# Scores of six half-sequences as 64-row matmuls in both row halves of TensorE, in three units of four PSUM banks

## The chip, the cores and the metric

One core of one Trainium2 chip runs the whole kernel. The metric is the device time of one execution in microseconds, median of several runs. The engines are named as in the profile: PE (TensorE matmuls), PEld (its weight loads), DVE (VectorE), ACT (ScalarE), POOL (GpSimd) and SP (SyncE, which here only issues DMAs).

## What is computed

Attention with a window of 96 keys and 8 global keys, with a linear bias per head, and behind it a gated feed-forward network (FFN) on the heads put side by side.

```python
batch, n_heads, seq, head_dim = (4, 8, 768, 64)
n_global, n_local = (8, 96)
...
scores = q @ k.T / sqrt(64) - slope[h] * dist
keep = (key < 8) | ((0 <= query - key) & (query - key < 96))
a = softmax(where(keep, scores, -1e9))
x = (a @ v), heads side by side            # 3072 x 512
out = (relu(x @ w_gate) * (x @ w_val)) @ w_out    # 512 -> 1536 -> 512
```

## The kernel before

**Tiling.** The 3072 queries are eight halves `s` of 384 (four sequences, two halves each); `s % 2` tells an even half from an odd one, and the halves three to eight of the title are `s` = 2 to 7. The keys lie in tiles of 120 with the 8 global keys ahead of them. Queries are taken in three interleaved sets (NN = 3), so a key tile that serves w positions makes 3w score columns per head. `banks_of_half` puts the key tiles that a half needs into three groups `g`, each a PSUM bank of scores for two heads: in an even half 432, 432 and 288 + 48 columns, in an odd one 144 + 336, 384 + 96 and 432 columns. The eight heads are four pairs `p`; a pair's q and k lie in 128 partitions, head `e` = 0 in the lower 64 and `e` = 1 in the upper 64.

**Scores before.** One matmul computes both heads of a pair: the weights are `kT` of the pair (128 rows), and the moving operand is a padded q (`qTb`) in which each head's columns have zeros in the other head's 64 rows. `piece_qk` (L396) does it for one group in one bank of `qk_psum`, puts the exponential on ACT (L413) and leaves the multiplication by the mask (`piece_mask`, L428, DVE) to be issued later.

**AV, normalization.** `piece_av` (L444) multiplies one head's exponentials by `vbuf`, which also holds ones, so the row sums come out beside the values; ACT takes their logarithm (L453) and, for both heads of a pair, the inverse as exp(-ln) (L458); `piece_norm` (L464, DVE) multiplies it into `xT`, the FFN's input. A head's exponentials of all its key tiles have to be there.

**Order of the work.** From half three on, the attention of half `c + 1` is woven by hand into the FFN of half `c`. `weave` (L769) walks through FFN items of equal weight (24 gate and value products, then the output products) and issues each attention item when its place has come; `spread` gives the places evenly. `attention_pieces` (L509) is the list: three banks of scores for pair 0, three for pair 1, the two AV of pair 0, and so on, 26 items. A stage has 35 FFN items, 31 where `c` = 6. Each engine then works strictly in the order of issue.

**PSUM.** Eight banks: three in `qk_psum`, two in `av_psum`, three in `ff_psum` (gate, value and output products). A gate's bank comes free with ACT's relu (L709), a value's bank with DVE's product (L716).

**Input of the halves four to eight.** `early_pieces` (L389) for half `c + 2`: POOL casts k into `kc` (L366) and q, with zeros between, into `qz` (L374); SP transposes them by DMA into `kNb` (L377) and `qTb` (L381); POOL orders the keys into `kT`. Half three is cast on POOL and transposed on PE in the setup weave (`T2_piece`, L942).

The heart of the scores before:

```python
ps = qk_psum.tile([128, 512], FP32, name="qk_ps")
...
nc.tensor.matmul(ps[:, c : c + n_], lhsT=kt[:, j, :],
                 rhs=qd[:, :, :, a : a + w], start=True, stop=True)
```

Of the kernel before, what the change touches and what calls it, by code (L numbers as in the profile page):

```python
# [8 lines left out]
FP32 = mybir.dt.float32  # L9
BF16 = mybir.dt.bfloat16  # L10
# [6 lines left out]
def kernel(  # L17
# [23 lines left out]
    NN = 3  # L41
# [24 lines left out]
    const = ctx.enter_context(tc.tile_pool(name="const", bufs=1))  # L66
    setupp = ctx.enter_context(tc.tile_pool(name="setupp", bufs=1))
    stage = ctx.enter_context(tc.tile_pool(name="stage", bufs=1))
    es_pool = ctx.enter_context(tc.tile_pool(name="es", bufs=3))
    rc_pool = ctx.enter_context(tc.tile_pool(name="rc", bufs=2))  # L70
    xt_pool = ctx.enter_context(tc.tile_pool(name="xt", bufs=3))
    ht_pool = ctx.enter_context(tc.tile_pool(name="ht", bufs=2))
# [14 lines left out]
    kT = [[const.tile([128, NT, 128], BF16, name=f"kT{i}_{p}") for p in range(HP)] for i in range(2)]  # L87
    qTb = [const.tile([128, HP, 2, QH], BF16, name=f"qT{i}") for i in range(2)]
    kNb = [const.tile([128, HP, QH], BF16, name=f"kN{i}") for i in range(2)]
    qz = [const.tile([128, NN, HP, 2, 128], BF16, name=f"qz{i}") for i in range(2)]  # L90
    kc = [const.tile([128, NN, DM], BF16, name=f"kc{i}") for i in range(2)]

    obuf = const.tile([128, 2, 5, DM // 2], FP32)
# [149 lines left out]
    def warm_up(n):  # L243
        wps = ff_psum.tile([128, 512], FP32, name="ff_ps")
        for _ in range(n):
            nc.tensor.matmul(wps, lhsT=warm, rhs=warm.unsqueeze(1).to_broadcast([128, 4, 128]), start=True, stop=True)

    xT_of = {}
    es_of = {}
    es01_of = {}  # L250
    av_of = {}

    cast_of = {}
# [91 lines left out]
    def piece_exp(s, p, g):  # L345
        if p == HP - 1:

            es = kNb[s].rearrange("d p t -> d (p t)")[:, 480 * g : 480 * (g + 1)]
        else:
            if g == 0:  # L350
                es01_of[s, p] = es_pool.tile([128, 2, 480], BF16, name="es01")
            es = es01_of[s, p][:, g] if g < 2 else es_pool.tile([128, 480], BF16, name="es2")
# [9 lines left out]
        for g in range(3):  # L362
            piece_exp(s, p, g)

    def piece_cast_k(s, p):
        nc.gpsimd.tensor_copy(  # L366
            kc[s % 2].rearrange("t n (h d) -> t h n d", d=D)[:, 2 * p : 2 * p + 2],
            ks_of[s][:, 2 * p : 2 * p + 2, :].rearrange("t e (n d) -> t e n d", n=NN))
# [7 lines left out]
    def piece_xk(s, n):  # L376
        nc.sync.dma_start_transpose(  # L377
            out=kNb[s % 2][:, :, n * 128 : (n + 1) * 128], in_=kc[s % 2][:, n])

    def piece_xq(s, n):  # L380
        nc.sync.dma_start_transpose(  # L381
            out=qTb[s % 2].rearrange("d p e t -> d (p e) t")[:, :, n * 128 : (n + 1) * 128],
            in_=qz[s % 2][:, n].rearrange("t p e z -> t (p e z)"))

    def piece_order(s, p):
        b, half = divmod(s, 2)
        put_keys(nc.gpsimd.tensor_copy, nc.gpsimd.tensor_copy, kT[b % 2][p], kNb[s % 2][:, p], half)

    def early_pieces(s):  # L389
        out = [(0.0, lambda p=p: piece_cast_k(s, p)) for p in range(HP)]  # L390
        out += [(0.0, lambda n=n: piece_xk(s, n)) for n in range(NN)]
        out += [(0.0, lambda p=p: piece_cast_q(s, p)) for p in range(HP)]
        out += [(0.0, lambda n=n: piece_xq(s, n)) for n in range(NN)]
        out += [(0.0, lambda p=p: piece_order(s, p)) for p in range(HP)]
        return out

    def piece_qk(s, p, g, later=None):
        b, half = divmod(s, 2)
        kt = kT[b % 2][p]
        qd = qTb[s % 2][:, p].rearrange("d e (n p) -> d e n p", n=NN)  # L400
        bank = banks_of_half[half][g]
        cols = sum(2 * NN * w for _, _, w, _ in bank)
        ps = qk_psum.tile([128, 512], FP32, name="qk_ps")
        if g == 0:
            es01_of[s, p] = es_pool.tile([128, 2, 480], BF16, name="es01")
        es = es01_of[s, p][:, g] if g < 2 else es_pool.tile([128, 480], BF16, name="es2")
        c = 0
        for j, a, w, m in bank:
            n_ = 2 * NN * w
            nc.tensor.matmul(ps[:, c : c + n_], lhsT=kt[:, j, :],  # L410
                             rhs=qd[:, :, :, a : a + w], start=True, stop=True)
            c += n_
        nc.scalar.activation(es[:, 0:cols], ps[:, 0:cols], AF.Exp, bias=0.0, scale=scale)  # L413
# [90 lines left out]
    def piece_mul_wide(s, p):  # L504
        if s not in xT_of:
            xT_of[s] = xt_pool.tile([128, N_DC, QH], BF16, name="xT")
        nc.vector.tensor_tensor(xT_of[s][:, p, :], av_of[s, p][1][:, 0:QH], av_of[s, p, "r"], op=ALU.mult)

    def attention_pieces(s):  # L509
        masks = []  # L510

        def qk(p, g):
            ready = masks[:]
            masks.clear()
            piece_qk(s, p, g, masks)
            for f in ready:
                f()

        def flush():
            for f in masks:  # L520
                f()
            masks.clear()

        QK = lambda p: [(0.18, lambda g=g: qk(p, g)) for g in range(3)]
        AV = lambda p: [(0.29, lambda e=e: (flush(), piece_av(s, p, e))) for e in range(2)]
        N = lambda p: [(0.0, lambda: piece_norm(s, p, 1))]
        g = QK(3)
        a = AV(2)
# [161 lines left out]
    def ffn_pieces(c):  # L690
# [63 lines left out]
        if c == NHALF - 2:  # L754
            return f1, pair.items({"1": late[0:2], "2": late[2:4]})

        space = qz[0].rearrange("t n p e z -> t (n p e z)").bitcast(FP16)
# [35 lines left out]

    for h in range(H):
        setup_sid(h)
    QKB, FFB, AVB = (qk_psum, "qk_ps"), (ff_psum, "ff_ps"), (av_psum, "av_ps")

    def AV(s, p, *pools):
        piece_av_wide(s, p, *pools)
        piece_norm_wide(s, p)  # L800
# [202 lines left out]
```

The softmax here doesn't subtract the row's maximum and nothing guards it: scores larger than these inputs give would overflow.

## Time and profile before

| | us |
|---|---|
| median of 7 runs | 242.06 (241.84 to 243.29) |
| the profiled execution | 242.33 |
| its span | 240.2 |
| granted TensorE clock, share of full | 1.0 in all slices |
| DMA | 32.37 MB, mean 135 GB/s |

The stages, by the start of each half's first gate product in the timeline of PE:

| stage | start | length | attention in it |
|---|---|---|---|
| FFN of half 3 (`c` = 2) | 77.46 | 26.68 | half 4 (odd) |
| `c` = 3 | 104.14 | 27.01 | half 5 (even) |
| `c` = 4 | 131.15 | 27.78 | half 6 (odd) |
| `c` = 5 | 158.93 | 27.00 | half 7 (even) |
| `c` = 6 | 185.93 | 25.09 | half 8 (odd) |
| `c` = 7 | 211.02 | to the end | none |

The attention of half 3 lies in the weave before 77 us, beside the last FFN items of the first two halves. In a row of the groups, the columns are the line, the engine, the operation, output and inputs with their shapes, the count; then the busy time, the mean duration of one, and the idle time of the engine just before them with what ended it. Durations of matmuls overlap: a matmul lasts until its last result is written, and the next one starts earlier.

### The profile page before, as it was taken

Reading aid. Unit: us, or ns where it says so; the run is one execution under the profiler, and the core shown is the slowest. Engines: PE = TensorE matmul, PEld = TensorE weight load, DVE = VectorE, ACT = ScalarE, POOL = GpSimd, SP = SyncE. Lnnn points to the kernel's source line nnn. Section 1 sums busy time; section 2 is a strip of 40 time slices with the busy share of each in tenths; the row PEclk is TensorE's granted clock in tenths of the full one; section 3 lists DMA queues with packets and bytes.
Section 4 is the critical chain, followed back from the end, with each engine's and each line's share of the span. In section 5 each row is a group of like instructions: output and inputs, shape, how many; then the busy total and the mean of one; then the engine's idle time right before and its main releaser. Section 6 shows DMA issues by size and latency. Waiting matters only on the chain.

```text
span 240.2 us, 5192 instructions
## 1 busy us (share of the span) xinstructions
PE 232.5 (97%) x1859; PEld 156.2 (65%) x1859; DVE 175.4 (73%) x443; ACT 154.5 (64%) x328; POOL 95.3 (40%) x213
## 2 busy tenths in 40 slices
PE   7889999999999999999999999999999999999993
PEld 4675765666558666776658666676658666766682
DVE  6877676767877769485895779675985867964783
ACT  7999855878662787538854787547764888433300
POOL 8998934924591068103484056502560000000000
PEclk9999999999999999999999999999999999999999
DMA  6999999997979956928659755929451200020004
GB/s 167 206 172 185 206 287 255 151 106 256 133 172 153 290 134 134 93 91 261 91 111 128 217 165 131 114 78 297 70 131 45 90 0 3 0 87 3 0 25 151
DMA packets 78329, 32.37 MB, mean 135 GB/s; under 512 B 55424, under 2 KB 76928, under 8 KB 78304
## 3 DMA queue, kind: packets, MB, share of 16 engines
q0 software_dynamic: 34896, 10.27, 38.1%
q1 hardware_dynamic: 43408, 21.78, 34.0%
q8 instruction: 14, 0.23, 0.4%
q14 instruction: 11, 0.09, 0.1%
HBM read 28.38 MB, written 6.29 MB: 144 GB/s over the span
## 4 chain that ended last, share of the span: by engine, by line
PE 81%; DMA 9%; POOL 6%; issue 2%; DVE 0%; POOLq 0%; DVEq 0%
PE ff_ps L700 46%; PE ff_ps L590 15%; PE ff_ps L733 9%; DMA ks<-in_k_dram 6%; PE av_ps L444 6%; PE qk_ps L410 6%; DMA vbuf<-in_v_dram 3%; POOL vbuf L151 1%; POOL kc L128 1%; POOL wg L168 1%; POOL qT L192 1%; PE qk_ps L296 1%; DVE obuf L601 0%; POOL obuf L260 0%; POOL wv L168 0%
## 5 line engine op out<-in xcount | busy, mean ns | idle before, releaser
L700 PE MATMUL ff_ps<-xT,wv 128*128 128x384 bf16 x384 | 77.7, 326 | 0.1
L700 PE MATMUL ff_ps<-xT,wg 128*128 128x384 bf16 x384 | 77.7, 326 | 0.0
L709 ACT ACTIVATE grelu<-ff_ps 128x384 bf16<-128x384 f32 x96 | 46.7, 490 | 45.5 <-PE ff_ps L700 32.9
L716 DVE TENSOR_TENSOR ht<-ff_ps,grelu 128x384 f16<-128x384 f32 x96 | 53.1, 554 | 24.5 <-PE ff_ps L700 12.4
L700 PEld LDWEIGHTS <-wv 128*128 128x128 bf16 x384 | 36.2, 97 | 22.4 <-DMA wv<-in_moe_w_val_dram 0.5
L700 PEld LDWEIGHTS <-wg 128*128 128x128 bf16 x384 | 36.0, 97 | 20.8 <-issue 0.5
L464 DVE TENSOR_TENSOR xT<-av_ps,rcp 64x384 bf16<-64x384 f32 x48 | 26.6, 555 | 24.8 <-ACT rcp L458 24.0
L413 ACT ACTIVATE es<-qk_ps 128x432 bf16<-128x432 f32 (+2 forms) x78 | 40.8, 532 | 5.7 <-PE qk_ps L410 3.7
L428 DVE TENSOR_TENSOR es<-es,m_all 128x432 bf16<-128x432 bf16 (+5 forms) x118 | 33.6, 329 | 0.2
L366 POOL CAST kc<-ks 128x384 bf16<-128x384 f32 x20 | 9.6, 525 | 57.6 <-DMA ks<-in_k_dram 57.6
L453 ACT ACTIVATE lnd<-av_ps 64x384 f32<-64x384 f32 x48 | 23.3, 485 | 9.0 <-PE av_ps L444 8.5
L410 PE MATMUL qk_ps<-qT,kT 128*128 128x432 bf16 (+5 forms) x118 | 26.6, 286 | 0.1
L151 POOL DMA_DIRECT2D vbuf<-in_v_dram x29 | 24.7, 861 | 0.1
L601 DVE TENSOR_TENSOR obuf<-ff_ps,obuf 128x512 f32<-128x512 f32 (+1 forms) x35 | 20.5, 592 | 4.4 <-PE ff_ps L590 2.1
L733 PE MATMUL ff_ps<-wo_sb,ht 128*128 128x512 f16 x96 | 22.8, 378 | 0.0
L444 PEld LDWEIGHTS <-vbuf 128*128 128x128 bf16 x216 | 18.3, 98 | 6.8
L444 PE MATMUL av_ps<-es,vbuf 128*128 128x216 bf16 (+4 forms) x216 | 21.4, 226 | 0.0
L590 PEld LDWEIGHTS <-hsum 128*128 128x128 f16 x168 | 16.4, 98 | 2.0
L410 PEld LDWEIGHTS <-kT 128*128 128x128 bf16 x118 | 11.4, 98 | 7.7
L590 PE MATMUL ff_ps<-wo_sum,hsum 128*128 128x256 f16 x126 | 14.9, 273 | 0.0
L590 PEld LDWEIGHTS <-ht 128*128 128x128 f16 x144 | 13.7, 97 | 1.8
L733 PEld LDWEIGHTS <-ht 128*128 128x128 f16 x96 | 8.7, 97 | 8.7
(125 smaller groups left out, 246.1 us busy)
## 6 DMA issues: line engine op xcount, KB each, us to landing
out_dram<-obuf SPq DMA_DIRECT2D x22, 256.0 KB
ks<-in_k_dram SPq DMA_DIRECT2D x5, 768.0 KB
qs<-in_q_dram SPq DMA_DIRECT2D x5, 768.0 KB
vbuf<-in_v_dram POOLq DMA_DIRECT2D x23, 120.0 KB, 4.6
wv<-in_moe_w_val_dram POOLq DMA_DIRECT2D x3, 512.0 KB, 9.8
wo_sb<-in_moe_w_out_dram POOLq DMA_DIRECT2D x1, 1536.0 KB, 21.8
wg<-in_moe_w_gate_dram POOLq DMA_DIRECT2D x2, 512.0 KB, 9.7
ks<-in_k_dram SPq DMA_DIRECT2D x4, 192.0 KB
```

Source lines behind the costliest of these rows:

```text
L151: nc.gpsimd.dma_start(out=v_dst(b, NG + r0, NG + r0 + n, j), in_=v[b, :, KT * j + r0 : KT * j + r0 + n, :].rearrange("h p d -> p h d"))
L410: nc.tensor.matmul(ps[:, c : c + n_], lhsT=kt[:, j, :], rhs=qd[:, :, :, a : a + w], start=True, stop=True)
L413: nc.scalar.activation(es[:, 0:cols], ps[:, 0:cols], AF.Exp, bias=0.0, scale=scale)
L428: nc.vector.tensor_mul(e4, e4, mk)
L444: nc.tensor.matmul(av3[:, :, a : a + w], lhsT=vb[:, j, z0 : z0 + 128], rhs=es[:, c : c + NN * w].rearrange("k (n p) -> k n p", n=NN), star ...
L453: nc.scalar.activation(ln[o0 : o0 + 64], av[d0 : d0 + 64, 0:QH], AF.Ln, bias=0.0, scale=1.0)
L464: nc.vector.tensor_tensor(xT_of[s][r, p, :], av_of[s, p, e][r, 0:QH], av_of[s, p, "r"][r], op=ALU.mult)
L590: nc.tensor.matmul(ps[:, c0 : c0 + DH], lhsT=lhs(i), rhs=rhs(i), start=(i == 0), stop=(i == NP - 1), skip_group_check=True)
L700: nc.tensor.matmul(st[key][:, 0:QH], lhsT=w_of(w, dc, fc), rhs=xT_of[c][:, dc, :], start=(dc == 0), stop=(dc == N_DC - 1))
L709: nc.scalar.activation(gr, psg[:, 0:QH], AF.Relu, bias=0.0, scale=1.0)
L716: nc.vector.tensor_tensor(ht[:, fc, :], psv[:, 0:QH], st["r", fc], op=ALU.mult)
L733: nc.tensor.matmul(ps2, lhsT=ht[:, fc, n * 128 : (n + 1) * 128], rhs=wo_sb[:, fc, :], start=(fc == 0), stop=(fc == N_FC - 1))
```

## The change

- The scores of the halves three to eight (`s` = 2 to 7) no longer use padded q. `score_unit` issues, for each key tile and pair, two matmuls of 64 rows: head `e` takes `kT` and q from the partitions 64e to 64e + 63, and so the rows 64e on of TensorE, and writes to a bank of its own. A bank now holds one head of each of two neighbouring pairs, with the same columns as before.
- Scores are issued in three units of four banks (two groups for both `e`), each one of `av_psum` and three of `qk_psum`. Unit 1 makes groups 0 and 1 of pairs 0 and 1; unit 2 their group 2 and group 0 of pairs 2 and 3; unit 3 the other two groups of pairs 2 and 3.
- `unit_exp` takes the exponential of one bank and leaves its mask to the next step; the list of `attention_pieces` puts the exponentials between the AV of pairs 0 and 1. It has 29 items, four of them empty ("wait").
- q is cast and transposed like k (`piece_cast2`, `piece_x`), without zeros; `qz` and its two memsets go, `qc` comes. The two transposed q buffers `qT2` lie in the one tile `qTb[1]`.
- Half three's q is copied for both heads in one ACT copy.
- `es_pool` has 12 buffers of one bank in place of 3 of two and 3 of one.
- The last attention is spread to 0.88 of its stage, as the others, in place of 0.8. The scratch space of the last output products lies in `qTb[0]`.

```diff
-    es_pool = ctx.enter_context(tc.tile_pool(name="es", bufs=3))
+    es_pool = ctx.enter_context(tc.tile_pool(name="es", bufs=12))
...
-    qz = [const.tile([128, NN, HP, 2, 128], BF16, name=f"qz{i}") for i in range(2)]
+    qT2 = [qTb[1].rearrange("d p e t -> d (p e t)")[:, i * HP * QH : (i + 1) * HP * QH].rearrange(
+        "d (p t) -> d p t", p=HP) for i in range(2)]
+    qc = [const.tile([128, NN, DM], BF16, name=f"qc{i}") for i in range(2)]
...
-    def piece_cast_q(s, p):
-        qsrc = qs_of[s][:, 2 * p : 2 * p + 2, :].rearrange("t e (n d) -> t e n d", n=NN)
-        for e in range(2):
-            nc.gpsimd.tensor_copy(qz[s % 2][:, :, p, e, 64 * e : 64 * e + 64], qsrc[:, e])
+    def piece_cast2(s, p, dst, src):
+        nc.gpsimd.tensor_copy(
+            dst[s % 2].rearrange("t n (h d) -> t h n d", d=D)[:, 2 * p : 2 * p + 2],
+            src[s][:, 2 * p : 2 * p + 2, :].rearrange("t e (n d) -> t e n d", n=NN))
+
+    def piece_x(dst, src, n):
+        nc.sync.dma_start_transpose(out=dst[:, :, n * 128 : (n + 1) * 128], in_=src[:, n])
...
+    def score_unit(s, groups, pools):
+        b, half = divmod(s, 2)
+        out = []
+        for pp, g in groups:
+            banks = []
+            for e in range(2):
+                pool, name = pools.pop(0)
+                banks.append(pool.tile([128, 512], FP32, name=name))
+                out.append((pp, g, e, banks[e]))
+            c = 0
+            for j, a, w, m in banks_of_half[half][g]:
+                for p in (2 * pp, 2 * pp + 1):
+                    for e in range(2):
+                        r = slice(64 * e, 64 * e + 64)
+                        q3 = qT2[s % 2][r, p].rearrange("d (n p) -> d n p", n=NN)
+                        nc.tensor.matmul(banks[e][:, c : c + NN * w], lhsT=kT[b % 2][p][r, j, :],
+                                         rhs=q3[:, :, a : a + w], start=True, stop=True)
+                    c += NN * w
+        return out
+
+    def unit_exp(s, pp, g, e, ps):
+        bank = banks_of_half[s % 2][g]
+        cols = sum(2 * NN * w for _, _, w, _ in bank)
+        es = es_pool.tile([128, 480], BF16, name="es")
+        nc.scalar.activation(es[:, 0:cols], ps[:, 0:cols], AF.Exp, bias=0.0, scale=scale)
+
+        def mask():
...
+                h0 = 4 * pp + e
+                mk = m_all[:, h0 : h0 + 3 : 2, 0 if j == 0 else 1, :, m : m + w]
...
+                nc.vector.tensor_mul(e4, e4, mk)
...
+        return mask
+
     def attention_pieces(s):
...
-        return (QK(0) + QK(1) + AV(0) + N(0) + QK(2) + AV(1) + N(1) + g[0:1] + a[0:1] + g[1:3] + a[1:2]
-                + N(2) + [(0.0, lambda: None)] * 2 + AV(3) + N(3))
+        def x(scored=None):
+            ready = masks[:]
+            masks.clear()
+            if scored:
+                scores(*scored)
+            masks.append(unit_exp(s, *units.pop(0)))
+            for f in ready:
+                f()
+
+        U = [([(0, 0), (0, 1)], (AVB, QKB, QKB, QKB)),
+             ([(0, 2), (1, 0)], (AVB, QKB, QKB, QKB)),
+             ([(1, 1), (1, 2)], (AVB, QKB, QKB, QKB))]
...
+        return (X(U[0]) + X() + X() + X() + wait + X(U[1]) + X() + a0[0:1] + X() + a0[1:2] + N(0) + X() + wait
+                + X(U[2]) + a1[0:1] + X() + a1[1:2] + N(1) + X() + X() + wait + AV(2) + N(2) + wait * 2 + AV(3) + N(3))
...
-    for i in range(2):
-        nc.gpsimd.memset(qz[i].rearrange("t n p e z -> t (n p e z)").bitcast(mybir.dt.uint32), 0)
...
-        piece_copy_q(2, p, nc.scalar.copy)
+        nc.scalar.copy(qT2[0][:, p], tp_of[2, p, 0])
...
-            placed.append(spread(attention_pieces(c + 1), 0.0, 0.88 if c + 2 < NHALF else 0.8))
+            placed.append(spread(attention_pieces(c + 1), 0.0, 0.88))
```

More of the change, by code (lines that the diff above doesn't have):

```diff
@@ L246, in warm_up @@
             nc.tensor.matmul(wps, lhsT=warm, rhs=warm.unsqueeze(1).to_broadcast([128, 4, 128]), start=True, stop=True)
+    QKB, FFB, AVB = (qk_psum, "qk_ps"), (ff_psum, "ff_ps"), (av_psum, "av_ps")
     xT_of = {}
     es_of = {}
-    es01_of = {}
     av_of = {}
@@ L349, in piece_exp @@
         else:
-            if g == 0:
-                es01_of[s, p] = es_pool.tile([128, 2, 480], BF16, name="es01")
-            es = es01_of[s, p][:, g] if g < 2 else es_pool.tile([128, 480], BF16, name="es2")
+            es = es_pool.tile([128, 480], BF16, name="es")
         c = 0
@@ L363, in piece_biased @@
             piece_exp(s, p, g)
-    def piece_cast_k(s, p):
+    def piece_cast2(s, p, dst, src):
         nc.gpsimd.tensor_copy(
-            kc[s % 2].rearrange("t n (h d) -> t h n d", d=D)[:, 2 * p : 2 * p + 2],
-            ks_of[s][:, 2 * p : 2 * p + 2, :].rearrange("t e (n d) -> t e n d", n=NN))
-    def piece_cast_q(s, p):
-        qsrc = qs_of[s][:, 2 * p : 2 * p + 2, :].rearrange("t e (n d) -> t e n d", n=NN)
-        for e in range(2):
-            nc.gpsimd.tensor_copy(qz[s % 2][:, :, p, e, 64 * e : 64 * e + 64], qsrc[:, e])
[L376 to L383, printed above, removed]
+            dst[s % 2].rearrange("t n (h d) -> t h n d", d=D)[:, 2 * p : 2 * p + 2],
+            src[s][:, 2 * p : 2 * p + 2, :].rearrange("t e (n d) -> t e n d", n=NN))
+    def piece_x(dst, src, n):
+        nc.sync.dma_start_transpose(out=dst[:, :, n * 128 : (n + 1) * 128], in_=src[:, n])
     def piece_order(s, p):
@@ L389, in early_pieces @@
     def early_pieces(s):
[L390 to L393, printed above, removed]
+        out = [(0.0, lambda p=p: piece_cast2(s, p, kc, ks_of)) for p in range(HP)]
+        out += [(0.0, lambda n=n: piece_x(kNb[s % 2], kc[s % 2], n)) for n in range(NN)]
+        out += [(0.0, lambda p=p: piece_cast2(s, p, qc, qs_of)) for p in range(HP)]
+        out += [(0.0, lambda n=n: piece_x(qT2[s % 2], qc[s % 2], n)) for n in range(NN)]
         out += [(0.0, lambda p=p: piece_order(s, p)) for p in range(HP)]
@@ L403, in piece_qk @@
         ps = qk_psum.tile([128, 512], FP32, name="qk_ps")
-        if g == 0:
-            es01_of[s, p] = es_pool.tile([128, 2, 480], BF16, name="es01")
-        es = es01_of[s, p][:, g] if g < 2 else es_pool.tile([128, 480], BF16, name="es2")
+        es = es_pool.tile([128, 480], BF16, name="es")
         c = 0
@@ L507, in piece_mul_wide @@
         nc.vector.tensor_tensor(xT_of[s][:, p, :], av_of[s, p][1][:, 0:QH], av_of[s, p, "r"], op=ALU.mult)
-    def attention_pieces(s):
[L510 to L517, printed above, removed]
+    def score_unit(s, groups, pools):
[20 more added lines that the diff above has]
+        cols = sum(2 * NN * w for _, _, w, _ in bank)
+        es = es_pool.tile([128, 480], BF16, name="es")
+        nc.scalar.activation(es[:, 0:cols], ps[:, 0:cols], AF.Exp, bias=0.0, scale=scale)
+        def mask():
+            c = 0
+            for j, a, w, m in bank:
+                n_ = 2 * NN * w
+                e4 = es[:, c : c + n_].rearrange("k (i n p) -> k i n p", i=2, n=NN)
+                h0 = 4 * pp + e
+                mk = m_all[:, h0 : h0 + 3 : 2, 0 if j == 0 else 1, :, m : m + w]
+                if w == WQ:
+                    e4 = e4.rearrange("k i n p -> k i (n p)")
+                    mk = mk.rearrange("k i n p -> k i (n p)")
+                nc.vector.tensor_mul(e4, e4, mk)
+                for i in range(2):
+                    es_of[s, 2 * pp + i, j, e] = (es, c + i * NN * w)
+                c += n_
+        return mask
+    def attention_pieces(s):
+        masks, units = [], []
         def flush():
@@ L522, in flush, with scores @@
             masks.clear()
-        QK = lambda p: [(0.18, lambda g=g: qk(p, g)) for g in range(3)]
-        AV = lambda p: [(0.29, lambda e=e: (flush(), piece_av(s, p, e))) for e in range(2)]
+        def scores(groups, pools):
+            units.extend(score_unit(s, groups, list(pools)))
+        def x(scored=None):
[9 more added lines that the diff above has]
+             ([(1, 1), (1, 2)], (AVB, QKB, QKB, QKB))]
+        X = lambda u=None: [(0.0, lambda: x(u))]
+        AV = lambda p: [(0.0, lambda e=e: (flush(), piece_av(s, p, e))) for e in range(2)]
         N = lambda p: [(0.0, lambda: piece_norm(s, p, 1))]
-        g = QK(3)
-        a = AV(2)
-        return (QK(0) + QK(1) + AV(0) + N(0) + QK(2) + AV(1) + N(1) + g[0:1] + a[0:1] + g[1:3] + a[1:2]
-                + N(2) + [(0.0, lambda: None)] * 2 + AV(3) + N(3))
+        wait = [(0.0, lambda: None)]
+        a0, a1 = AV(0), AV(1)
+        return (X(U[0]) + X() + X() + X() + wait + X(U[1]) + X() + a0[0:1] + X() + a0[1:2] + N(0) + X() + wait
+                + X(U[2]) + a1[0:1] + X() + a1[1:2] + N(1) + X() + X() + wait + AV(2) + N(2) + wait * 2 + AV(3) + N(3))
     out_v = out.rearrange("(s p n) d -> s n p d", p=128, n=NN)
@@ L755, in ffn_pieces @@
             return f1, pair.items({"1": late[0:2], "2": late[2:4]})
-        space = qz[0].rearrange("t n p e z -> t (n p e z)").bitcast(FP16)
+        space = qTb[0].rearrange("d p e t -> d (p e t)").bitcast(FP16)
         across = Pair((c - 1, 2), (c, 2), space.rearrange("t (s c z) -> t s c z", s=4, c=NP))
@@ L795 @@
         setup_sid(h)
-    QKB, FFB, AVB = (qk_psum, "qk_ps"), (ff_psum, "ff_ps"), (av_psum, "av_ps")
     def AV(s, p, *pools):
```

## The prediction

> **What bounds the kernel now.** I read the page first: how busy each engine is, the chain that ended last, the groups of the lines that the change touches.
>
> ```profile
> PE 232.5 (97%) x1859; PEld 156.2 (65%) x1859; DVE 175.4 (73%) x443; ACT 154.5 (64%) x328; POOL 95.3 (40%) x213
> ...
> PE 81%; DMA 9%; POOL 6%; issue 2%; DVE 0%; POOLq 0%; DVEq 0%
> ...
> L413 ACT ACTIVATE es<-qk_ps 128x432 bf16<-128x432 f32 (+2 forms) x78 | 40.8, 532 | 5.7 <-PE qk_ps L410 3.7
> ...
> L410 PE MATMUL qk_ps<-qT,kT 128*128 128x432 bf16 (+5 forms) x118 | 26.6, 286 | 0.1
> ```
>
> TensorE (PE) is busy 97% and makes 81% of the chain; what isn't PE in it lies in the first 40 us, where nothing is changed. Asked from 47 us on, the list of waits holds no wait of PE at all. So from there to the end a microsecond of PE time is a microsecond of the kernel, as long as no new wait arises. A busy sum can't price a matmul, because consecutive matmuls overlap (432 columns last 0.35 us but the next starts 0.18 us later); I price by the distance from one start to the next, in PE's timeline:
>
> ```profile
> 133.70 0.35 PE L410 MATMUL qk_ps<-qT,kT 128*128 128x432 bf16 x1
> 133.88 0.81 PE L700 MATMUL ff_ps<-xT,wv 128*128 128x384 bf16 x4
> 134.53 0.81 PE L700 MATMUL ff_ps<-xT,wg 128*128 128x384 bf16 x4
> 135.18 0.37 PE L410 MATMUL qk_ps<-qT,kT 128*128 128x144 bf16 x2
> 135.39 0.33 PE L700 MATMUL ff_ps<-xT,wv 128*128 128x384 bf16 x1
> ```
>
> Four FFN products of 384 columns take 0.65 us, so 162.5 ns each, which is 2.5 ns and 1 ns per 2.4 columns. By that 432 columns take 182.5 ns (the rows: 0.18) and the bank of 144 and 336 takes 205 (the rows: 0.21).
>
> **What the scores cost now.** Per pair of heads an even half has 432, 432, 288 and 48 columns: 182.5 + 182.5 + 122.5 + 28 (the 48 columns by the start of the next product, 109.69 to 109.72 us) = 515 ns. An odd half has 144, 336, 384, 96 and 432: 62.5 + 142.5 + 162.5 + 42.5 + 182.5 = 592. Four pairs, three halves of each sort: 12 x 0.515 + 12 x 0.592 = 13.3 us.
>
> **What they cost in row halves.** No 64-row product stands in this trace. The nearest row is L479, the AV of the first two halves, which puts two heads side by side in *column* halves:
>
> ```profile
> 25.73 0.48 PE L479 MATMUL qk_ps<-es,ones 128*64 128x72 bf16 x10
> 26.04 0.48 PE L479 MATMUL qk_ps<-es,vbuf 128*64 128x72 bf16 x10
> 26.45 1.47 PE L700 MATMUL ff_ps<-xT,wv 128*128 128x384 bf16 x8
> 27.76 0.81 PE L700 MATMUL ff_ps<-xT,wg 128*128 128x384 bf16 x4
> 28.50 0.50 PE L479 MATMUL av_ps<-es,ones 128*64 128x72 bf16 x10
> 28.84 0.48 PE L479 MATMUL av_ps<-es,vbuf 128*64 128x72 bf16 x10
> ```
>
> Ten matmuls, five pairs of 72, 168, 192, 48 and 216 columns, take 0.31 us (25.73 to 26.04). One after the other they would take 0.58 us for the columns alone. So both matmuls of a pair run at once, at the price of one. The columns per head in an odd half are just these five: 0.308 us for two heads. In an even half (216, 216, 144, 24) it is 92.5 + 92.5 + 62.5 + 28 = 276 ns. Over all: 12 x 0.308 + 12 x 0.276 = 7.0 us, **6.3 us less**.
>
> **What going in and out of the halves costs.** The same rows show it. The ten matmuls from 26.04 should be followed at 26.35; L700 comes at 26.45, and its eight products then take 1.31 instead of 1.30: 0.11 us to leave the mode. On the way in, the four products from 27.76 stream until 28.41, L479 starts at 28.50, and its first ten take 0.34 instead of 0.31: 0.12 us. The other entry, at 25.08, gives 0.12 as well. In the kernel before the halves from three on never change mode. The change has three units in each of six halves, all between 128-row products: 18 entries and 18 exits, 18 x 0.12 + 18 x 0.11 = **4.1 us more**. Two thirds of the gain go here. I take the same price for row halves; the bounds are nothing (switching rows costs no gap) and twice that.
>
> **The weights.** There are twice as many loads, 64 rows by 128 columns. In L479 a pair's two loads of 64 columns fit between pairs 25 ns apart; a 128x128 load fits into the 28 ns of a 24-column product. So 128 columns for both row halves fit in 28 ns if they load together (cost nothing: every pair is at least that long), and in 56 ns if one after the other. Then only the pairs of 24, 48 and 72 columns grow, by 28, 28 and 24 ns: 12 x 28 + 12 x 52 = 1.0 us. I take 0, the L479 row, and keep 1.0. A page of the Trainium skill speaks against the 6.3 us ("TensorE: Matmul & The Clock Gate", Part 3, Measured speedup): four row tiles gave 3.07 times, not four. By that the 7.0 us would be 7.0 / 0.77 = 9.1, the gain 4.2, and switching would eat all of it; the rows above show pairs at full rate, and I go by them.
>
> **New waits.** PE works in order, so a unit that waits for one of its four banks holds up the FFN behind it. An attention item comes after about 1.06 FFN products of 0.65 us (29 items on 0.88 x 35; before, 26). I walked an even half from its start at 0, with relu 0.49, exponential 0.53 to 0.58, mult 0.55 and Ln 0.49 us as in ACT's and DVE's rows, and 0.2 us from a product's last start of a bank to its reader.
> - Unit 1 at 0.65 needs three qk banks and an AV bank, all long free. Its four exponentials share ACT with three relus and end at 4.35.
> - Unit 2 (after the sixth product, 4.45) needs the qk banks of the second to fourth exponential; the last is wanted by its second group alone, at 4.75. Slack 0.35 us.
> - AV of pair 0 (6.3) needs the mask after unit 2's first exponential, done at about 6.1 on DVE. Slack 0.2; before, it needed masks from two banks earlier. This is the tightest place.
> - Unit 3 (11.4) needs an AV bank whose normalization ends near 10.8, and an exponential that ends near 11.4, again for its second group alone. Slack 0.3. AV of pair 1 needs nothing of unit 3.
> - The exponentials now take the AV banks too, but in the walk each is read 0.6 us or more before it is asked for again.
>
> ACT could turn these slacks into stalls, since everything above hangs on it. Its share in the first 24 products of each stage (columns: PE, weight loads, DVE, ACT):
>
> ```profile
> 104.14:123.43 19.29, 19.29 (x138) 12.27 (x136) 15.07 (x37) 14.52 (x31) 6.82 (x19) 1.00 0.69 172
> 131.15:151.14 19.99, 19.96 (x148) 12.80 (x146) 16.18 (x41) 15.16 (x31) 8.33 (x24) 1.00 0.68 171
> ...
> 186.05:206.59 20.54, 20.54 (x159) 13.45 (x157) 16.16 (x44) 16.65 (x34) 0.00 (x0) 1.00 0.08 27
> ```
>
> 75 to 81%. Exponentials and masks keep their number and sizes, so the same work goes into some 0.35 us less: 77 to 83%. No lasting backlog; I put 0.4 us in all for the tight places (bounds 0 and 2.4, the latter 0.4 us in each half). Below nothing this can't go, as PE waits for nothing now.
>
> **Edits at nothing.** The padded q casts (8 of 0.38 us per half on POOL) become 4 of 0.53, the size of the kc rows: POOL works 0.9 us less in each half at 40% load, and nothing but the transposes waits for it. The q transposes stay three DMAs on SP's queue (4.26 us, as for the k ones of half the width), behind the k ones and ahead of only the result stores; in the stage from 104 us they end at 122.3 and their reader starts at 131. Both q buffers now lie in one tile; were it tracked whole, a transpose would wait for unit 3, which is a quarter of a stage earlier. The two memsets (2.7 us) go from in front of POOL's 5.6 us wait for ks and only lengthen that wait. Half three's q copies are four on ACT, not eight (0.47 each), while PE waited there for a cast. Twelve es buffers only remove waits. Spreading the last attention to 0.88 puts its last AV five products ahead of the FFN that needs it, as in the other stages, where the norm ends at 130.27 and the product starts at 131.15: 0.9 us of cover, and what exceeds it would be paid once.
>
> **The sum.** -6.3 + 4.1 + 0 + 0.4 = -1.8 us. The profiled execution has a span of 240.2 and a time of 242.33, 2.1 outside the span, which nothing here touches: 238.4 and 240.5. The median is 242.06, 0.3 below that execution; on it, **240.3 us**. A change can be told from none beyond 0.3%, 0.73 us: 241.33 and 242.79 are the bounds.
>
> **Rivals.**
> 1. *Nothing lost at the switches* (6%). The drain seen is that of column halves; with row halves at no gap the sum is -6.3 + 0.4: 236.2. Against it: PE's outgoing weights must be replaced in all rows either way.
> 2. *The waits take it back* (20%). ACT runs late at unit 2, at AV of pair 0 and unit 3. For it: DVE and ACT already wait on one another (24.0 us of norms on rcp, 6.7 of mults on exponentials), and slack is 0.2 to 0.35 us. At its bound of 2.4 us the sum is +0.2: 242.3. It decides from 0.37 us per half. From that price to half as much again (3.3 us), 241.5 to 243.2.
> 3. *The row halves don't run side by side* (12%). Two matmuls with separate inputs write all 128 partitions of two banks at once, which no row here does; L479 writes 64 each. If they take turns, the columns are as many as before, 13.3 us, and 108 more starts at 2.5 ns add 0.3: the switches come on top, 4.1 + 0.3 + 0.4 = +4.8, **246.9, slower**. It decides from 2.2 us over 108 pairs, 20 ns a pair: at 20 ns above L479's distance the gain is gone. Slower weight loads are the same mechanism, smaller.
>
> **How the numbers follow.** The forecast has 62%: with the loads at 1.0, and waits from 0 to 0.8, it spans 239.9 to 241.7; with switches a fifth cheaper, 239.1. Of its 62, 57 are faster and 5 the same. Rival 1 gives 6 faster; rival 2 gives 2 faster, 11 the same, 7 slower; rival 3, which can be partial, 1 the same and 11 slower. In all 65 faster, 17 the same, 18 slower. The range of 8 in 10 leaves out rival 1 and the full rival 3: 238.8 to 243.2.
>
> **What would show it.** In PE's timeline, score matmuls of 64 rows in pairs 3 ns apart and 92 ns to the next for 216 columns (right) or about 185 (rival 3); some 0.1 us of gap at each edge of a unit (none: rival 1); new waits of PE on es, xT or exponentials from 47 us on, over 2 us in sum (rival 2). The stage from 104.14 to 131.15, 27.0 us, should become 26.7. A forecast of faster is wrong if the pairs are 20 ns late or the waits pass 0.37 us in a half.

## The result, and the profile after

| | before | after |
|---|---|---|
| median, us | 242.16 (31 runs) | 244.21 (243.62 to 245.47, 12 runs) |
| ratio | | 1.0089, 95% interval 1.0075 to 1.0104 |
| span of the profiled execution, us | 240.2 | 241.9 |

The changed kernel is 0.9% slower; 240.3 had been forecast, 0.7% faster. The page of the changed kernel, engines, chain and the groups that answer to those shown of before (scores are L513 and L522 now, AV is L431):

```profile
PE 232.8 (96%) x1967; PEld 152.9 (63%) x1967; DVE 175.4 (73%) x443; ACT 149.2 (62%) x324; POOL 88.2 (36%) x191
...
PE 78%; DVE 9%; ACT 8%; issue 2%; DMA 1%; SPq 0%; DVEq 0%; ACTq 0%
...
L431 PE MATMUL av_ps<-es,vbuf 128*128 128x216 bf16 (+4 forms) x216 | 23.8, 226 | 1.3 <-DVE es L534 1.0
```

The busy sums hardly move, and PE's would tell nothing anyway, since its durations overlap. The chain tells more, though not by these shares alone: DVE and ACT held 0% of it and now hold 17%, 40 us, but 17 of the 40 lie ahead of 47 us, in the setup, where the chain of before ran over DMA and POOL. From 47 to 232 us the chain before was PE alone; now DVE holds 15.7 us of that stretch and ACT 4.5. And AV now waits for `es`; before, it waited for nothing:

```profile
L444 PE MATMUL av_ps<-es,vbuf 128*128 128x216 bf16 (+4 forms) x216 | 21.4, 226 | 0.0
```

The list of waits from 47 us to the end, PE and its weight loads, which was empty but for 0.7 us, is now (columns: who waited for whom, us in all, times, longest):

```profile
PE av_ps L431 <- DVE es L534: 1.0, 4, 0.3
```

```profile
PEld L513 <- issue: 4.1, 13, 0.3
PEld L741 <- issue: 4.1, 22, 0.3
PEld L431 <- issue: 1.8, 6, 0.4
PEld L513 <- DVE ht L757: 1.6, 5, 0.3
```

These lists count only idle time that a record shows whole, and "issue" hides who was late. I therefore added up the distances between matmul starts, beyond what the columns take (1 ns per 2.4 columns and 2.5 ns), from 47 us on. That gives the sum by its terms:

| term, us over six halves | forecast | in the trace after |
|---|---|---|
| scores (13.3 before) | 7.0, so -6.3 | 7.17 in 18 units, so -6.1 |
| gaps into and out of the units | +4.1 | 1.72 + 1.63, and 0.2 at the product behind: +3.5 |
| waits of PE | +0.4 | AV 3.6, gate and value products 1.2, output products 0.25, less 0.4 that stood there before: +4.6 |
| sum | -1.8 | +2.0 |

The span grew by 1.7 rather than 2.0: half three's k landed 0.9 us earlier in this execution (its first cast on POOL starts at 37.04 instead of 37.94), and a PE wait of 0.5 us at 40.47 is gone. The starts bear the sum out: the last gate product ahead of the first unit starts 0.64 us earlier than before (46.26), PE's last product of all 1.49 us later, 2.1 us in between.

**The score unit** works as forecast. PE in the stage of half 5, from 104.16 us:

```profile
104.16 0.81 PE L741 MATMUL ff_ps<-xT,wg 128*128 128x384 bf16 x4
104.90 0.26 PE L513 MATMUL av_ps<-qT,kT 64*128 64x216 bf16 x1
104.91 0.26 PE L513 MATMUL qk_ps<-qT,kT 64*128 64x216 bf16 x1
105.01 0.25 PE L513 MATMUL av_ps<-qT,kT 64*128 64x216 bf16 x1
105.01 0.44 PE L513 MATMUL qk_ps<-qT,kT 64*128 64x216 bf16 x5
105.38 0.82 PE L741 MATMUL ff_ps<-xT,wv 128*128 128x384 bf16 x4
```

Two products of 64 rows start together, into banks of their own, and the next two 0.1 us later. The products from 104.16 stream until 104.81, and the unit starts at 104.90: the gap of 0.1 us in; the gap out is alike.

**Where it is lost** is 17 us further on, at the AV of pair 2. PE, ACT and DVE (POOL and the weight loads are left out):

```profile
120.08 1.13 DVE L451 TENSOR_TENSOR xT<-av_ps,rcp 64x384 bf16<-64x384 f32 x2
...
120.90 0.49 ACT L750 ACTIVATE grelu<-ff_ps 128x384 bf16<-128x384 f32 x1 [0.18 <-PE ff_ps L741]
...
121.25 0.56 DVE L757 TENSOR_TENSOR ht<-ff_ps,grelu 128x384 f16<-128x384 f32 x1
121.29 0.44 ACT L522 ACTIVATE es<-qk_ps 128x336 bf16<-128x336 f32 x1
121.44 0.81 PE L741 MATMUL ff_ps<-xT,wg 128*128 128x384 bf16 x4
...
121.72 0.51 DVE L626 TENSOR_TENSOR hsum<-ht 128x512 f16<-128x512 f16 x1
...
122.09 0.35 PE L431 MATMUL av_ps<-es,vbuf 128*128 128x216 bf16 x2
122.16 0.69 DVE L534 TENSOR_TENSOR es<-es,m_all 128x288 bf16<-128x288 bf16 x2
...
122.72 0.34 PE L431 MATMUL av_ps<-es,vbuf 128*128 128x144 bf16 x2 [0.28 <-DVE es L534]
...
122.77 0.55 DVE L757 TENSOR_TENSOR ht<-ff_ps,grelu 128x384 f16<-128x384 f32 x1
...
123.23 0.41 DVE L627 TENSOR_TENSOR hsum<-ht,hsum 128x512 f16<-128x512 f16 x1
...
123.56 0.39 DVE L534 TENSOR_TENSOR es<-es,m_all 128x288 bf16<-128x288 bf16 x2
123.57 0.61 PE L431 MATMUL av_ps<-es,vbuf 128*128 128x216 bf16 x4
```

AV of head 0 of pair 2 starts at 122.09 with its first two products, then stands for 0.45 us until the mask of unit 3's third bank is through; head 1 starts at 123.57 and stands for 0.16 us for the mask of the fourth, which DVE begins at 123.56. The last exponential ended at 121.73, so the masks are late on DVE and not on ACT: behind two normalizations, value products (L757) and FFN sums (`hsum`). DVE in the same stretch before the change:

```profile
122.45 0.54 DVE L586 TENSOR_TENSOR hsum<-ht,hsum 128x512 f16<-128x512 f16 x1
122.91 0.40 DVE L428 TENSOR_TENSOR es<-es,m_all 128x432 bf16<-128x432 bf16 x1
123.43 0.56 DVE L716 TENSOR_TENSOR ht<-ff_ps,grelu 128x384 f16<-128x384 f32 x1
123.90 0.61 DVE L428 TENSOR_TENSOR es<-es,m_all 128x288 bf16<-128x288 bf16 x2
```

The masks were no earlier there: the last began at 123.90. But they belonged to pair 3, whose AV came at 126.02. In the new layout a bank holds one head of two pairs, so the last banks' masks are wanted by AV of pair 2 as well, more than two microseconds sooner.

How full DVE's queue is there, from 117.18 to 124.43 us (columns: the stretch, PE, weight loads, DVE, ACT, POOL, clock, DMA): 6.89 of 7.25 us, where the stages as wholes have 72 to 79%.

```profile
117.18:124.43 7.25, 6.96 (x49) 4.20 (x48) 6.89 (x17) 5.15 (x12) 5.09 (x15) 1.00 0.34 74
```

The gates lose the rest: the gate product ahead of unit 3 starts 0.09 us late in five halves and 0.24 us in half eight, the one ahead of AV of pair 2 in five (in the rows above, at 121.44 and not 121.35). By the timeline it wants a bank of `ff_psum`: the relu of the gate before runs from 120.90 to 121.39, and the product starts 0.05 later.

### The profile page after: what moved, and what is told of

Same layout as the page of the kernel before. It is cut to its first block, busy times and chain, and to the rows that moved or that the text cites. A ratio compares the mean times of both kernels' runs of the same rounds, so it can differ in the third digit from the quotient of the medians.

```text
span 241.9 us, 5381 instructions
## 1 busy us (share of the span) xinstructions
PE 232.8 (96%) x1967; PEld 152.9 (63%) x1967; DVE 175.4 (73%) x443; ACT 149.2 (62%) x324; POOL 88.2 (36%) x191
## 4 chain that ended last, share of the span: by engine, by line
PE 78%; DVE 9%; ACT 8%; issue 2%; DMA 1%; SPq 0%; DVEq 0%; ACTq 0%
PE ff_ps L741 45%; PE ff_ps L631 14%; PE ff_ps L774 7%; PE av_ps L431 6%; PE av_ps L513 2%; ACT es L359 2%; DVE xT L451 2%; DVE ht L757 2%; DVE es L534 2%; PE qk_ps L513 2%; DMA qs<-in_q_dram 1%; DVE obuf L642 1%; ACT grelu L750 1%; ACT obuf L263 1%; DVE hsum L626 1%
## 5 line engine op out<-in xcount | busy, mean ns | idle before, releaser
L757 DVE TENSOR_TENSOR ht<-ff_ps,grelu 128x384 f16<-128x384 f32 x96 | 53.3, 556 | 27.1 <-PE ff_ps L741 21.2
L534 DVE TENSOR_TENSOR es<-es,m_all 128x432 bf16<-128x432 bf16 (+3 forms) x108 | 32.6, 339 | 0.7 <-ACT es L522 0.7
L522 ACT ACTIVATE es<-qk_ps 128x432 bf16<-128x432 f32 (+2 forms) x54 | 27.7, 528 | 0.0
L431 PE MATMUL av_ps<-es,vbuf 128*128 128x216 bf16 (+4 forms) x216 | 23.8, 226 | 1.3 <-DVE es L534 1.0
L431 PEld LDWEIGHTS <-vbuf 128*128 128x128 bf16 x216 | 18.3, 98 | 7.5 <-issue 1.8
L774 PE MATMUL ff_ps<-wo_sb,ht 128*128 128x512 f16 x96 | 22.3, 378 | 0.0
L445 ACT ACTIVATE rcp<-lnd 128x384 f32<-128x384 f32 x24 | 12.5, 523 | 0.8
L631 PE MATMUL ff_ps<-wo_sb,ht 128*128 128x256 f16 x96 | 12.8, 272 | 0.1
```

The lines of the kernel that those rows point to most:

```text
L431: nc.tensor.matmul(av3[:, :, a : a + w], lhsT=vb[:, j, z0 : z0 + 128], rhs=es[:, c : c + NN * w].rearrange("k (n p) -> k n p", n=NN), star ...
L534: nc.vector.tensor_mul(e4, e4, mk)
L631: nc.tensor.matmul(ps[:, c0 : c0 + DH], lhsT=lhs(i), rhs=rhs(i), start=(i == 0), stop=(i == NP - 1), skip_group_check=True)
L757: nc.vector.tensor_tensor(ht[:, fc, :], psv[:, 0:QH], st["r", fc], op=ALU.mult)
L774: nc.tensor.matmul(ps2, lhsT=ht[:, fc, n * 128 : (n + 1) * 128], rhs=wo_sb[:, fc, :], start=(fc == 0), stop=(fc == N_FC - 1))
```

## The experiments

The theories are called in them as they were when they were written: W, the waits are the loss and sit at AV of pairs 2 and 3; its rivals R, S and others as told there. All times are medians, the ratio is to the kernel before on the same chip.

### Moving the AV of pair 2

```diff
-... X() + X() + wait + AV(2) + N(2) + wait * 2 + AV(3) + N(3))
+... X() + X() + wait * 2 + AV(2) + N(2) + wait + AV(3) + N(3))
```

> The changed kernel with one edit: of the empty places behind AV of pair 2 one is put ahead of it, so AV of pairs 2 moves back by one attention item (1.06 FFN products, 0.7 us); pair 3 stays. Theory W (the loss is PE waiting inside AV of pairs 2 and 3 for masks that DVE reaches late, 3.6 us over six halves, and 1.1 us of gate products waiting for a bank): the 3.6 us fall below 1, the time falls by 2.5 to 3.5 us, to 240.7 to 241.7. Rival R (DVE is short of time as a whole in these stages, so the wait only moves to the next reader): less than 0.7 us gained, 243.5 to 244.2. Rival S (the row halves and their switches cost more than they save, waits aside): some gain, but not below the kernel before, 242.2 or more.

244.2 us, ratio 1.008 (1.0063 to 1.0097): nothing gained. AV's own waits fall in four halves out of six, but grow in halves three and eight (3.1 us are left of 3.6), and the output products now start 1.1 us late. In the stage from 104.79 us:

```profile
123.37 0.42 PE L431 MATMUL av_ps<-es,vbuf 128*128 128x216 bf16 x4
124.00 0.81 PE L774 MATMUL ff_ps<-wo_sb,ht 128*128 128x512 f16 x3 [0.21 <-DVE ht L757]
124.65 0.64 PE L431 MATMUL av_ps<-es,vbuf 128*128 128x216 bf16 x4
```

```profile
124.20 0.55 DVE L757 TENSOR_TENSOR ht<-ff_ps,grelu 128x384 f16<-128x384 f32 x1
124.67 0.39 DVE L534 TENSOR_TENSOR es<-es,m_all 128x288 bf16<-128x288 bf16 x2
```

The output product waits for the last value product, and head 1's AV again for its mask, which the item of head 0's AV itself puts into DVE's queue (`flush`): moved with AV, it now stands behind one more value product. So the queue behind DVE is late as a whole at this place, whoever reads first. W's remedy was wrong, and R holds in so far; that DVE is short over the whole stage is tested next.

### Taking the sums out of the queue

```diff
-            if c > 1 and 7 <= fc < N_FC - 1:
+            if False:
...
-        late = pair.sums(0 if c == 1 else 4, NP)
+        late = pair.sums(0, NP)
```

> The changed kernel with one edit: the four sums of FFN activations that DVE makes behind value products 8 to 11 (0.42 us each, four per half) are made whole with the later ones, in the output part of the stage. Theory W: they stand in DVE's queue just ahead of the last masks, so without them the masks of pairs 2 and 3 come up to 1.2 us earlier and most of the 3.6 us goes: 241 to 242.3. Rival R' (what holds the masks up is ACT: exponentials late behind relus and logarithms): no change within 0.5 us, 243.7 to 244.7. If the later sums (0.6 us each) hold up the output products, PE waits there instead, up to 0.5 us per half.

241.55 us, ratio 0.9968 (0.9951 to 0.9986): 2.7 us less than the changed kernel and below the kernel before. AV's waits fall from 3.6 to 1.3 us, of which 0.7 are in half three, whose stage has sums of weights that this edit leaves. DVE and PE at the AV of pair 2, in the same stage as above:

```profile
122.23 0.76 DVE L534 TENSOR_TENSOR es<-es,m_all 128x288 bf16<-128x288 bf16 x2
122.91 0.55 DVE L757 TENSOR_TENSOR ht<-ff_ps,grelu 128x384 f16<-128x384 f32 x1
123.38 0.39 DVE L534 TENSOR_TENSOR es<-es,m_all 128x288 bf16<-128x288 bf16 x2
```

```profile
122.64 0.58 PE L431 MATMUL av_ps<-es,vbuf 128*128 128x216 bf16 x4
...
123.72 0.42 PE L431 MATMUL av_ps<-es,vbuf 128*128 128x216 bf16 x4
```

The last mask now begins 0.34 us ahead of head 1's AV. The same DVE work, now done after 126 us and not between 117.8 and 123.6, costs next to nothing. So DVE is not short of time in the stage, as R had it, it is late in one stretch; and R' (ACT holds the masks up) falls with the 2.7 us.

The control, the same edit in the kernel before:

> The kernel before with the same late sums, for control. Its PE waits for nothing there, so moving the sums can gain nothing: 242.0 to 242.6 (theory); if the late sums hold up output products by themselves, up to 0.5 us more. Rival: the gain seen with late sums in the changed kernel has nothing to do with the new order, and shows here too: 239.0 to 240.5.

242.74 us, ratio 1.0019 (1.0003 to 1.0035): no gain, rather a small loss, and the group of the late products shows its place, 0.8 us of waiting for a sum:

```profile
L590 PE MATMUL ff_ps<-wo_sum,hsum 128*128 128x256 f16 x126 | 14.9, 273 | 0.8 <-DVE hsum L584 0.8
```

It stands in the stage with 31 items, where the output products follow at once. The gain belongs to the new order.

### The order without row halves

Scores as 128-row products over padded q, in the new units and the new list:

```diff
-                        r = slice(64 * e, 64 * e + 64)
-                        q3 = qT2[s % 2][r, p].rearrange("d (n p) -> d n p", n=NN)
-                        nc.tensor.matmul(banks[e][:, c : c + NN * w], lhsT=kT[b % 2][p][r, j, :],
+                        q3 = qTb[s % 2][:, p, e].rearrange("d (n p) -> d n p", n=NN)
+                        nc.tensor.matmul(banks[e][:, c : c + NN * w], lhsT=kT[b % 2][p][:, j, :],
```

> The kernel before with the new order alone: three units of four banks, the new list of attention items, 0.88 for all halves; scores still as 128-row products over padded q, one head per product of up to 216 columns, so 13.3 us plus 108 more starts, and no switch of mode. es has nine buffers. Theory W: the waits belong to the order; PE has some 0.5 us more work per half as cover, so 1 to 3 us of waits, 243.3 to 245.5. Rival S (the loss is the row halves' own): no waits, 242.1 to 242.7.

247.51 us, ratio 1.0229 (1.0184 to 1.0274). The order alone costs 5.3 us, more than expected: the starts of its PE are late by 3.7 us in AV, 1.2 in gates and 0.3 in output products. More PE work was no cover: AV waits as long as in the changed kernel. (That the masks hang on exponentials, which then come later too, would explain it; it was not tried.) S falls: the loss is in the order, and the row halves win back 3.3 of it.

### Both normalizations together

The first normalization of a pair is issued right behind the second AV and waits at the head of DVE's queue for the inverse; here, besides the late sums, it is issued with the other at N:

```diff
             av_of[s, p, "r"] = rc
-            piece_norm(s, p, 0)
...
-        N = lambda p: [(0.0, lambda: piece_norm(s, p, 1))]
+        N = lambda p: [(0.0, lambda: (piece_norm(s, p, 0), piece_norm(s, p, 1)))]
```

> The changed kernel with the sums made late (as before in this study), and besides with both normalizations of a pair issued together at its N item, not the first one right behind the second AV. What is left of waits with the late sums is, per half, two gate products 0.09 us late and 0.1 to 0.2 us in AV of pairs 2 and 3, over six halves 2 us. Theory W': the first normalization waits for the inverse at the head of DVE's queue and holds up the value product behind it, and so its bank; issued one item later it doesn't: the two 0.09 us go, and the time falls by 0.5 to 1.5 us against late sums alone, to 240.1 to 241.1. Rival: the gates wait for ACT's relu of the gate before, whatever DVE does: no gain, 241.3 to 241.9.

240.38 us, ratio 0.9924 (0.9905 to 0.9943): 1.2 less than with late sums alone. The gate ahead of unit 3 is on time in every half, the one ahead of AV of pair 2 still 0.09 late; for that one the rival, ACT's relu, holds. DVE at the AV of pair 2, and a stretch like the one above:

```profile
120.62 0.56 DVE L756 TENSOR_TENSOR ht<-ff_ps,grelu 128x384 f16<-128x384 f32 x1
121.09 0.66 DVE L533 TENSOR_TENSOR es<-es,m_all 128x288 bf16<-128x288 bf16 x2
121.68 0.54 DVE L756 TENSOR_TENSOR ht<-ff_ps,grelu 128x384 f16<-128x384 f32 x1
122.15 0.39 DVE L533 TENSOR_TENSOR es<-es,m_all 128x288 bf16<-128x288 bf16 x2
122.76 0.56 DVE L756 TENSOR_TENSOR ht<-ff_ps,grelu 128x384 f16<-128x384 f32 x1 [0.22 <-ACT lnd L440]
```

```profile
116.59:123.32 6.73, 6.73 (x50) 4.25 (x49) 5.27 (x13) 5.29 (x12) 4.33 (x14) 1.00 0.36 80
```

The sums are gone from between, DVE is busy 5.27 of 6.73 us and waits for others again, and PE is busy throughout. The same edit without the sums:

> The changed kernel with both normalizations of a pair at its N item, and the four early sums left where they are. Theory: two causes stand side by side in DVE's queue. The first normalization costs the gates ahead of unit 3 and part of the backlog; the sums the rest. So about half of the gain of late sums and normalizations together (244.2 to 240.4): 241.5 to 243. Rival (the sums alone make the backlog, the order of the normalizations matters only once they are gone): 243.4 to 244.2.

242.78 us, ratio 1.0033 (1.0013 to 1.0053). So the four versions are 244.2, 242.8 (normalizations), 241.55 (sums) and 240.4 (both): the two gains, 1.4 and 2.7, nearly add up (4.1, and 3.8 for both). AV still loses 3.4 us with the normalizations alone; what went are the gates ahead of unit 3 and 0.5 us in half three.

### What the row halves are worth with the waits gone

> The new order with padded q and 128-row products (no switch of mode), with late sums and both normalizations at the N item: what the row halves by themselves are worth where hardly anything waits. Theory, by the trace of the changed kernel: the units cost 7.2 us in row halves and 3.35 us of gaps at their edges, against 13.3 and 0.3 for more starts: the padded kernel is 3.0 us slower than the same with row halves (240.4), less up to 0.5 us of waits that its longer products cover: 242.8 to 243.5. Rival (the row halves bring nothing net, and the gain lies in sums and normalizations): 240.2 to 241.2.

243.84 us, ratio 1.0076 (1.0047 to 1.0105), 3.5 us above the same with row halves; 2.4 to 3.1 had been expected. Its PE still waits 1.7 us, the one with row halves 1.6, so the difference is PE work: 13.5 - 7.2 - 3.5 = 2.8 by the starts. The spans of the two profiled executions, 241.3 and 238.6, say the same; what the medians have beyond it lies within the spread of the four runs (243.38 to 244.77).

### The price of a switch, and the pairing

With late sums, one product of 24 columns and 128 rows between the two groups of each unit:

```diff
+            if pp == groups[0][0] and g == groups[0][1]:
+                nc.tensor.matmul(banks[0][:, 480:504], lhsT=ident, rhs=ident[:, 0:24], start=True, stop=True)
```

> The changed kernel with late sums, and in each unit, between its two groups, one 128-row product of 24 columns into columns 480 to 503 of a bank, which nobody reads: 18 more exits from the 64-row mode and 18 more entries. Theory: each costs what the gaps in the trace of the changed kernel show, 96 ns in and 91 out, with up to 20 ns behind each, and the small product its 28: 18 x 0.215 to 0.255 = 3.9 to 4.6 us, so 245.2 to 246.3 against 241.55. Rival: the gap is mostly the wait of the first product after longer ones and not a price per switch: under 2 us more, below 243.5.

245.41 us, ratio 1.0135 (1.0107 to 1.0163): 3.9 us more than without. Gaps in were 1.72 and are 3.35 us (28 ns taken for the small product itself), gaps out 1.63 and 3.29, so the price is paid per switch, wherever it stands.

The pairing was tried twice. First, in the changed kernel, head 0's products of a group ahead of head 1's:

```diff
-            for j, a, w, m in banks_of_half[half][g]:
-                for p in (2 * pp, 2 * pp + 1):
-                    for e in range(2):
+            for e in range(2):
+                c = 0
+                for j, a, w, m in banks_of_half[half][g]:
+                    for p in (2 * pp, 2 * pp + 1):
```

> The changed kernel with the products of a group ordered by head: all of head 0's (rows 0 to 63), then all of head 1's (rows 64 to 127), so neighbours in the queue use the same rows, but for one pair at the boundary. Same switches, same banks. If the row halves run side by side only when neighbours use different rows, score time doubles: about 5.5 us more PE work, of which the masks' waits take up 1 to 3: 246.5 to 249.5. If the two heads never ran at once or run at once whatever the order, no change: 243.7 to 244.7.

245.15 us, ratio 1.0117 (1.0089 to 1.0146). A miss, and not conclusive: the units grow only from 7.17 to 7.38 us, and the waits in AV by 0.5. With two or four products per head in a group, the end of one run still lies beside the start of the next. So, with late sums, the whole unit by head:

```diff
+        for e in range(2):
+            for pp, g, _, ps in out[e::2]:
+                c = 0
+                for j, a, w, m in banks_of_half[half][g]:
+                    for p in (2 * pp, 2 * pp + 1):
```

> The changed kernel with late sums, and in each unit all products of head 0 in both groups first, then all of head 1, so that neighbours in the queue use the same rows but for one pair per unit. With the order by head inside each group alone, the last and first products of successive runs still fell beside each other, and only 0.9 us were lost. Theory: scores cost nearly 13.3 us again less one pair per unit (18 x 0.06 to 0.09), so 4.5 to 5.5 us more PE work than side by side; a little of it is cover for waits: 245.2 to 247. Rival (products of different rows need not be neighbours to run at once): under 1.5 us more, 241.5 to 243.

244.45 us, ratio 1.0092 (1.0062 to 1.0121): 2.9 us more than in pairs, and the units take 10.03 us, not 7.17. Side by side is worth real time, but still less is lost than expected; the section on the hardware shows why.

### A mixed version

```diff
-            if False:
+            if c == NHALF - 2 and 7 <= fc < N_FC - 1:
...
-        late = pair.sums(0, NP)
+        late = pair.sums(4 if c == NHALF - 2 else 0, NP)
```

> The changed kernel with late sums and both normalizations at the N item, but for the stage with 31 items, where the sums stay early: there the output products follow at once and waited 0.4 us for late sums (0.25 and 0.1 us, and 0.08 at the next stage). 239.9 to 240.5, below both kernels; against the version with all sums late 0.2 to 0.4 us less. Rival: in that stage too the early sums hold up masks by as much, 240.3 to 240.8.

240.38 us, ratio 0.993 (0.9906 to 0.9954). The time lies in both ranges, but nothing is gained on the version with all sums late, where 0.2 to 0.4 us had been expected, and so the rival held: early sums in that one stage hold up masks (0.28 us in AV) by about as much as late ones hold up output products. The version with late sums and both normalizations at N stays as good as any here, 0.8% below the kernel before.

## Why the prediction was wrong

- **Bound.** Right: PE had no slack after 47 us, and the late starts that were added up, +2.0 us, are what the median grew by (2.05). (Not all that isn't PE in the chain before lies in the first 40 us: 1.2 us of DVE stand at its very end.)
- **Scores in row halves.** Right: 7.17 us where 7.0 was forecast. That two 64-row products write all 128 partitions at once with next to no loss was taken from column halves and holds; rival 3 falls. The estimate of 9.1 us, worked out from the Trainium skill's figure for four row tiles ("TensorE: Matmul & The Clock Gate", Part 3, Measured speedup), is not what two row tiles show here.
- **Switches.** Right in kind and size: 96 ns in, 91 out, 3.5 us for 36 with the products behind, where 4.1 was forecast; rival 1 falls. The reason held against it, that the weights must be replaced in all rows either way, explains nothing: each FFN product has weights of its own too, and they follow one another after 162.5 ns without a gap. What makes the gap stays open.
- **Weights, casts, transposes, `es`.** Right: no wait of PE in the trace leads to them.
- **0.88.** Not settled. In the one stage that it changes, an output product starts 0.25 us late (208.81 us), behind a value product that stands behind two normalizations in DVE's queue (207.03 to 208.17). Whether 0.8 would have spared that was not tried.
- **New waits: the step that failed.** "I put 0.4 us in all for the tight places (bounds 0 and 2.4, the latter 0.4 us in each half)": it is 4.6 us, 0.8 per half. Two things went wrong in it. The walk followed the new list to AV of pair 1 and stopped; AV of pair 2 was not looked at, though the new banks make it need unit 3's last masks. The three places that were walked hardly wait (AV of pair 0 in half three alone, 0.26 us). And the load was judged by ACT's mean share of 75 to 81% over 24 products. The queue that was late is DVE's, in one stretch: 0.36 us idle in 7.25. With most of these waits taken out (late sums, normalizations together) 1.6 us are left, and the median is 240.38, next to the 240.3 of the forecast: the other terms stood, within some 0.4 us. A smaller slip lies in the walk's 0.2 us from a product's last start to its reader: in the traces it is 0.21 and 0.22 behind products of 24 and 48 columns, but 0.29 behind 216 and 0.38 behind 432.
- **Rival 2** had the right mechanism, waits that take the gain back, from 0.37 us per half on, but named other places, put the blame on ACT first, and priced it at up to 3.3 us where it is 4.6. Its range is also off at the lower end: by the forecast's own terms the 2.2 us at which it decides give 242.1, not 241.5.

Shown by runs: the late queue (late sums, both with and without the new order), its second cause (normalizations), the price of a switch, and the worth of the row halves. That a bank for two pairs makes AV of pair 2 wait is read from the two traces; a layout with one pair per bank was not tried.

## What to carry to other kernels

A new layout changes who needs which result when: for each reader in the new order, to the last one, write down its last input and where that stands in the queue of the engine that makes it. A mean share of an engine over a stage says nothing of a stretch in which its queue runs without a gap; there, issue later what nobody waits for. And if a reader is moved back, look whether the work that it waits for is issued by the reader's own item and moves back with it.

## What the hardware did that I had not expected

Products of different row halves need not be neighbours in the queue to run at once. With a whole unit ordered by head, head 1's first product starts while three of head 0's, issued before it, have not begun. Starts in us of one unit of `heads_apart`, by the order of issue, eight products for each head:

```
head 0   72: 133.399, 133.438   168: 133.472, 133.547   192: 133.619, 133.702    48: 133.784, 133.813
head 1   72: 133.628, 133.666   168: 133.700, 133.775   192: 133.848, 133.930    48: 134.013, 134.041
```

Head 1's product of 72 columns starts at 133.628, 9 ns after head 0's first of 192, and ahead of head 0's second of 192 and both of 48. The trace's starts alone might be a matter of its model, but the time agrees: units of 10.03 us and 2.9 us in all, where taking turns would have cost 4.5 or more. The Trainium skill ("TensorE: Matmul & The Clock Gate", Part 3, The mechanism) says that matmuls keep the order of the queue in start and end; for the two row halves this trace shows otherwise, and the measurement decides. So what stands ahead of the prediction, that each engine works strictly in the order of issue, does not hold for PE here.
